# A tile's rounding, the signs of others and some sums of blocks change places between block 0 and block 2

## The chip, the cores and the metric

The kernel runs on one core of a Trainium2 chip. The core has five engines that run beside each other, each through its own list of instructions in order: TensorE (PE, matrix products), VectorE (DVE), ScalarE (ACT), GpSimd (POOL) and SyncE (SP, which here only issues DMAs). They wait for one another through semaphores. The metric is the device time of one execution in microseconds, as the median of several runs.

## What is computed

Linear attention over 8 batches of 8 heads (576 positions, 64 dimensions) is normalised, its heads are laid side by side into x (4608 x 512), and a two-layer network with a leaky ReLU follows:

```python
kv = np.einsum('bhsd,bhse->bhde', k, v)
out = np.einsum('bhsd,bhde->bhse', q, kv)
rms = np.sqrt(np.mean(out * out, axis=-1, keepdims=True) + 1e-06)
x = (out / rms * g_norm)        # heads side by side: 4608 x 512
h = x @ w_in                    # 512 x 2048
g = np.maximum(0.01 * h, h)
out = g @ w_out                 # 2048 x 512
```

q, k, v and the result are float32. w_in and w_out arrive as float64 and are rounded to float32 on the chip.

## The kernel before

**Blocks and units.** The 4608 rows of x are nine blocks of 512. The hidden width of 2048 is four chunks c = 0 to 3. Block 0 is computed for its first three chunks in a plain way (`first_block`, 12 steps: product h_ps, the ReLU L1139 on ACT, then product o_acc one step later). Then comes a list of units, each one chunk of one block: block 1 with chunks 0 to 3 (units 0 to 3), block 0 with chunk 3 (unit 4), and then blocks 2 to 8 with four chunks each. A unit computes both matrix products by Strassen's scheme, seven products in place of eight, in the order 1, 2, 6, 5, 7, 3, 4 (`ORDER`). Products 5, 6, 7 and 3 or 4 need sums of operand blocks: those of w_in (`sides_w1`, on POOL, into `pairs`), of x (`sides_x`, on DVE), of g (`sums_of`, on POOL, into `gs`) and of w_out (`sides_w2`, on POOL). From block 2 on the first product is split by Strassen a second time; the sums for that come from `combine` (POOL, into `stage`, then by DMA to a copy in DRAM) and from `inner` (POOL).

**The loop and its slots.** Each unit has seven slots t = 0 to 6, one for each product of h. In a slot the generator of h gives one product (PE, and the instruction on ACT or DVE that reads it); two slots behind, the generator of o gives one of the unit before. After that the slot issues stored-up DMAs (`write_later`), sums on POOL (`combine`), pieces of a tile's rounding, loads, and pieces of the attention for later blocks (`a_steps`). Nearly all instructions are pinned, so that the order of the lines is the order on each engine, and DMAs on SP are issued in that order too.

**Rounding.** The weights come as 32 tiles of 128 x 512 float64 values (`w_jobs`). One tile's rounding (`round_f64`) is a chain across two engines: ACT add (L264), ACT cut (L262), DVE clamp (L266), ACT sign and scale (L271, "the sign" below), DVE L281, DVE L284. It is a generator with a stop after each of these and one empty stop ahead of L271. In block 0, `round_w` takes the first three steps and leaves the rest to `finish_w`, written as f in the plan of steps; a number in the plan is a tile, a is one step of block 1's attention, t one of its leftover from block 0, and x makes all four sums of block 1's x at once (L1174). In a plan key (n, half), half 0 stands before the o_acc of the step before, half 1 after it. Tiles 27 to 31 are rounded in the loop, three slots each. A tile is loaded by SP into one of a few places (`early`, `stage`, `pairs`) once an earlier tile there has been read.

**POOL's entry into block 1.** L1193 copies one element of x's last sum into `pairs`, so POOL begins block 1 only when the four sums are done. It then makes, in order: the four sums of w_in for unit 0, two of w_out, eight for combine(0, 0) and combine(0, 1), two more of w_out; and then within the loop those of the next unit.

Of the kernel before, what the change touches and what calls it, by code (L numbers as in the profile page):

```python
# [24 lines left out]
def kernel(  # L25
# [754 lines left out]
    def combine(c, part):  # L780


        direct = w1_sb[0][c].rearrange("p u (t r) m -> p u r t m", t=2)
        last = w1_sb[1][c][:, :, 2:, :].unsqueeze(3)
        parts = [((5, 6), pair(0, U, 2, 2, P))], [((7, 3), pair(1, U, 2, 2, P))], \
            [((1, 2), direct), ((4,), last)]

        for js, y in parts[part]:
            t = view(next(stage_homes), 0, 4, len(js), P)
            s1, s2, s3, s4 = (t[:, i, :, :] for i in range(4))  # L790
            y11, y12, y21, y22 = (y[:, u, r, :, :] for u in range(2) for r in range(2))

            add(nc.gpsimd, s1, y21, y22)
            add(nc.gpsimd, s2, s1, y11, True)
            add(nc.gpsimd, s3, y11, y21, True)
            add(nc.gpsimd, s4, y12, s2, True)
            to = w1_dram[c][:, :, AT[js[0]]:AT[js[0]] + len(js), :]
            if js[0] == 1:
                for r in range(2):
                    put_off(to[:, r, :, :], y[:, 0, r, :, :], 2 - part // 2)  # L800
            else:
                put_off(to[:, :2, :, :], y[:, 0, :, :, :], 2 - part // 2)
            put_off(to[:, 2, :, :], y22, 2 - part // 2)
            put_off(to[:, 3:, :, :], t, 2 - part // 2)
# [291 lines left out]
    def go(steps, n=None):  # L1096
        while n is None or n > 0:
            if next(steps, steps) is steps:
                return
            n = None if n is None else n - 1  # L1100
# [20 lines left out]
    def first_block(between):  # L1121
# [27 lines left out]
        for t in range(4):  # L1149
# [10 lines left out]
    plan = {(1, 0): (5, f, t), (1, 1): (t, 6, f, t), (2, 0): (t, 7, f, t), (2, 1): (8, f, t, t),  # L1160
            (3, 0): (9, f, t, a), (3, 1): (10, f), (4, 0): (11, f, a), (4, 1): (12, f),
            (5, 0): (13, f, a), (5, 1): (14, f), (6, 0): (15, f), (6, 1): (16, f),
            (7, 0): (a, a, 17, f), (7, 1): (a, 18, f), (8, 0): (a, 19, 24, f), (8, 1): (a, 20, f),
            (9, 0): (a, a, 21, f), (9, 1): (22, a, f, a), (10, 0): (a, 23, f, a), (10, 1): (x, 25, f),
            (11, 0): (26, f)}
    loaded, x_sides = 12, None

    def between(n, half):
        nonlocal loaded, x_sides
        for what in plan.get((n, half), ()):  # L1170
            if what == f:
                finish_w()
            elif what == x:
                x_sides, _, sums, _ = sides_x(1)  # L1174
                go(sums)
            elif what in (t, a):
                go(tail if what == t else a_steps, 1)
            else:
                round_w(what)
                to = what + 7 if what < 17 else {23: 26, 25: 28, 26: 28}.get(what, 25)  # L1180
                while loaded <= min(to, 31):
                    load_w(loaded)
                    loaded += 1
                    if loaded in (13, 16):
                        load_pair(1, {13: 2, 16: 3}[loaded], homes=homes_1[{13: 2, 16: 3}[loaded]])
# [11 lines left out]
    for part in range(2):  # L1197
# [2 lines left out]
    in_loop = True  # L1200

    LATE_ONE = {15: 2, 16: 2, 17: 1, 18: 1, 19: 2}
    A_SLOTS = {18: 1, 19: 2, 22: 1, 23: 1, 24: 1, 25: 1, 26: 1, 27: 1, 28: 2, 29: 1, 30: 1, 31: 2,
               34: 2}
    DIRECT = {23: 0, 25: 1, 27: 2, 29: 3}
    READS = {28: 2, 30: 4, 32: RING}
# [27 lines left out]
    for i, chunks in rounds:  # L1234
        one = in_block_1 = i < 2
        steady = not one
        if i == 1:
            late, a_steps = a_steps, attention(2)
        elif i > 1:
            late, a_steps = a_steps, attention(i + 1, fine=True) if i + 1 < B else iter(())  # L1240
        os = {}
        for c in chunks:
            now += 1
            nxt = units[now + 1] if now + 1 < len(units) else (NB, 0)
            g_sides = {}
            h_steps = product_h(now, h_sides, x_sides, g_sides) if one else \
                product_h_two(i, c, now, quarters, g_sides, second_of(now - 2))
            for t in range(7):
                slot = 7 * c + t
                if rest:  # L1250
                    go(steps, rest[0][0])
                go(h_steps, 1)
                if not one:

                    if t == 6:
                        go(h_steps, 1)
                    if slot in LATE_SLOTS:
                        go(late, 1)
                    for _ in range(FINE_SLOTS.get(slot, 0)):
                        go(a_steps, 1)  # L1260
                    if i + 1 < NB:
                        if slot == 20:
                            x_sides, new_quarters, sums, inner = sides_x(i + 1)
                        if slot in (20, 21, 22):
                            go(sums, 2 if slot == 20 else 1)
                        if slot == 24:
                            inner(0)
                        elif slot == 25:
                            inner(1)
                    load_some()  # L1270

                if now - 1 in seconds:
                    for half in range(2):
                        if t == (6 if half else 4):
                            inner_g(now - 1, half)
                    if t == 5 and now - 1 < 2 * NC + NC - K:
                        inner_w2(units[now - 1][1])
                if (7 * now + t == 7 * NC + 4):
                    while writes:
                        pin(nc.sync.dma_start(*writes.pop()))  # L1280
                if slot in HELD and i == NB - 1:
                    pass
                elif waited == LAG:
                    go_o()
                elif o_queue:
                    waited += 1
                write_later()
                at = 7 * now + t
                for key in PARTS.get(at, ()):
                    if at == 33:  # L1290
                        part_os = os
                    load_part(part_os, key)
                if at in READS:
                    read(READS[at])
                if one:
                    if at in DIRECT:
                        combine(DIRECT[at], 2)
                    if t == 3 and nxt[0] < 2 and nxt[1] != c:
                        h_sides, more_h = sides_w1(nxt[1])
                        combine(nxt[1], 0)  # L1300
                    if t == 5 and nxt[0] < 2 and nxt[1] != c:
                        more_h()
                        combine(nxt[1], 1)
                    if not rest and rounded < len(w_jobs):
                        steps = rounding(rounded)
                        rest.extend(((0, 3), (2, 1), (0, 1)))
                        rounded += 1
                    if rest:
                        go(steps, rest.popleft()[1])
                    if loaded < min(rounded + 2, len(w_jobs)):  # L1310
                        load_w(loaded)
                        loaded += 1
                    if at in (15, 16):
                        load_pair(2, at - 15)
                    go(late, LATE_ONE.get(at, 0))
                    go(a_steps, A_SLOTS.get(at, 0))
                    load_some(2 if at in (19, 20) else 1)
                    if at == 7 * NC - 4:
                        x_sides, _, sums, _ = sides_x(0)
                    elif at == 7 * N1 - 3:  # L1320
                        x_sides, new_quarters, sums, inner = sides_x(2)
                    if at in (7 * NC - 4, 7 * NC - 3, 7 * N1 - 3, 7 * N1 - 2):
                        go(sums, 2)
                    if at == 7 * N1 - 2:
                        inner(0)
                    elif at == 7 * N1 - 1:
                        inner(1)

            for _ in range(2 if i == NB - 1 and c == NC - 1 else 0):
                go(h_steps, 1)  # L1330
                go_o()
            go(h_steps)
            if c == NC - 1 and i != 1 and i + 1 < NB:
                inner(2)
                quarters = new_quarters
            by_two = NC + NC - K <= now < len(units) - 2
            if by_two:
                seconds[now] = (os, store(i))
            o_queue.append(product_o(now, g_sides, os, store(i), by_two))
# [32 lines left out]
```

## Time and profile before

| | us |
|---|---|
| median of 3 runs | 929.04 |
| lowest and highest | 926.89, 932.18 |
| the profiled execution's own time | 930.66 |
| its span, first to last instruction | 929.0 |
| PE busy | 910.7 (98%) |
| DVE busy | 610.2 (66%) |
| ACT busy | 347.5 (37%) |
| POOL busy | 390.6 (42%) |

The granted clock of TensorE was 0.994 of full speed in the mean. PE is busy nearly all the time, so the profile is read for the few places where it isn't, and for what ends each of those waits. A busy PE that runs at a lower granted clock counts as busy too, so the length of a group of products has to be compared with that of its like. In a row of the timeline the first number is the start, the second the length to the last visible end; a bracket gives the idle time of the engine before it and what ended that.

### The profile page before, as it was taken

What the parts mean: (1) busy time and instruction counts of PE and PEld (TensorE: products, weight loads), DVE (VectorE), ACT (ScalarE), POOL (GpSimd) and SP (SyncE); (2) the same over time, 40 slices, a digit from 0 to 9 for tenths busy, and PEclk for the clock granted to TensorE, in tenths of its full rate; (3) what the DMA queues carried; (4) which work ended last, traced back from release to release, by engine and by line L of the source; (5) the groups of instructions that cost most, each with busy time, mean ns of one, the idle gap of its engine ahead of it and who ended that gap; (6) DMA issues with size and microseconds to landing.
All of it is one profiled execution on the core that took longest, in us unless ns stands there. A gap on an engine that the chain in (4) does not pass through costs nothing.

```text
span 929.0 us, 18151 instructions
## 1 busy us (share of the span) xinstructions
PE 910.7 (98%) x7024; PEld 785.7 (85%) x7024; DVE 610.2 (66%) x1119; ACT 347.5 (37%) x679; POOL 390.6 (42%) x475
## 2 busy tenths in 40 slices
PE   8999798999999999999999999999999999999998
PEld 4544367888898999999999999999999999999997
DVE  5765872554565877577756785688658755765565
ACT  5756543213334422433243324433343333223330
POOL 2000189898452275226322632254325522552322
PEclk9999999999999999999999999999999999999999
DMA  8998255797989678867886788757765676667633
GB/s 252 230 249 215 68 196 185 206 301 224 292 273 324 224 227 252 261 218 234 245 263 224 226 206 270 241 168 223 240 185 172 192 223 198 184 188 218 198 119 91
DMA packets 92405, 202.16 MB, mean 218 GB/s; under 512 B 10016, under 2 KB 44448, under 8 KB 92320
## 3 DMA queue, kind: packets, MB, share of 16 engines
q1 hardware_dynamic: 81344, 189.14, 69.0%
q10 hardware_dynamic: 10528, 10.69, 3.4%
q8 instruction: 56, 0.92, 0.4%
q0 software_dynamic: 448, 1.18, 0.3%
q14 instruction: 29, 0.24, 0.1%
HBM read 173.44 MB, written 27.53 MB: 216 GB/s over the span
## 4 chain that ended last, share of the span: by engine, by line
PE 82%; DMA 9%; POOL 3%; DVE 3%; issue 1%; ACT 1%; SPq 0%; POOLq 0%; ACTq 0%; DVEq 0%
PE o_c L126 19%; PE o_a L126 18%; PE h_ha L126 11%; PE h_hb L126 10%; PE h_hc L126 8%; PE h_hd L126 8%; DMA pairs<-in_moe_w_in_dram 3%; PE o_ps L126 3%; DMA stage<-in_moe_w_in_dram 2%; POOL stage L698 2%; PE h_a L126 2%; POOL pairs L698 1%; PE h_c L126 1%; DMA pairs<-in_v_dram 1%; PE h_b L126 1%
## 5 line engine op out<-in xcount | busy, mean ns | idle before, releaser
L698 POOL TENSOR_TENSOR gs<-g 128x512 f32<-128x512 f32 x66 | 84.3, 1278 | 249.1 <-ACT g L909 249.1
L909 ACT ACTIVATE g<-g 128x512 f32<-128x512 f32 x127 | 80.1, 631 | 143.0 <-DVE g L698 143.0
L1028 ACT COPY w_all<-h_ha 128x512 f32<-128x512 f32 x84 | 48.9, 582 | 171.3 <-PE h_ha L126 165.6
L126 PE MATMUL o_a<-pairs,gs 128*128 128x256 f32 x392 | 93.6, 381 | 2.6 <-POOL gs L698 2.6
L126 PE MATMUL o_c<-pairs,gs 128*128 128x256 f32 x392 | 93.2, 381 | 0.0
L698 DVE TENSOR_TENSOR o<-o_a,o 128x512 f32<-128x512 f32 (+1 forms) x93 | 62.7, 674 | 34.3 <-PE o_a L126 33.8
L698 DVE TENSOR_TENSOR o<-h_hb,o 128x128 f32<-128x128 f32 x104 | 29.9, 287 | 83.0 <-ACT pairs L1028 82.9
L126 PEld LDWEIGHTS o_a<-pairs,gs 128*128 128x128 f32 x392 | 71.4, 191 | 11.0 <-POOL gs L698 3.0
L126 PEld LDWEIGHTS o_c<-pairs,gs 128*128 128x128 f32 x392 | 71.3, 190 | 9.5 <-POOL pairs L698 1.2
L698 DVE TENSOR_TENSOR o<-o_c,o 128x512 f32<-128x512 f32 x80 | 54.8, 685 | 32.9 <-PE o_c L126 32.7
L126 PE MATMUL h_ha<-stage,w_all 128*128 128x128 f32 x448 | 59.9, 276 | 1.7 <-POOL stage L698 1.7
L126 PEld LDWEIGHTS h_ha<-stage,w_all 128*128 128x128 f32 x448 | 56.7, 192 | 4.8 <-POOL stage L698 1.9
L698 DVE TENSOR_TENSOR g<-g,pairs 128x512 f32<-128x512 f32 x84 | 55.7, 689 | 1.9
L698 POOL TENSOR_TENSOR pairs<-g 128x128 f32<-128x128 f32 x52 | 23.7, 456 | 77.1 <-PE h_hb L126 48.5
L126 PE MATMUL o_acc<-w,g 128*128 128x512 f32 x96 | 46.7, 632 | 6.0 <-ACT g L1139 6.0
L698 DVE TENSOR_TENSOR w_all<-h_hc,w_all 128x512 f32<-128x512 f32 x56 | 38.4, 685 | 15.8 <-PE h_hc L126 15.8
L698 DVE TENSOR_TENSOR o<-h_hd,o 128x128 f32<-128x128 f32 x78 | 22.2, 284 | 38.1 <-ACT pairs L1028 38.0
L126 PE MATMUL h_hb<-stage,w_all 128*128 128x128 f32 x336 | 46.7, 275 | 0.0
L698 POOL TENSOR_TENSOR gs<-gs,g 128x512 f32<-128x512 f32 x33 | 44.5, 1348 | 2.6
L1028 ACT COPY pairs<-h_hb 128x384 f32<-128x384 f32 x84 | 40.0, 476 | 13.6 <-PE h_hb L126 13.1
L1193 POOL COPY pairs<-xt 1x1 f32<-1x1 f32 x1 | 0.2, 177 | 106.7 <-DVE xt L698 106.7
L698 POOL TENSOR_TENSOR gs<-g,gs 128x512 f32<-128x512 f32 x33 | 45.0, 1362 | 0.0
(237 smaller groups left out, 2273.9 us busy)
## 6 DMA issues: line engine op xcount, KB each, us to landing
w_all<-w SPq DMA_DIRECT2D x196, 448.0 KB, 4.2
pairs<-w SPq DMA_DIRECT2D x56, 512.0 KB, 4.3
out_dram<-o ACTq DMA_DIRECT2D x35, 256.0 KB, 4.6
v_in<-in_v_dram SPq DMA_DIRECT2D x27, 288.0 KB, 4.7
k_in<-in_k_dram SPq DMA_DIRECT2D x26, 288.0 KB, 4.4
q_in<-in_q_dram SPq DMA_DIRECT2D x52, 144.0 KB, 5.5
q_in<-in_q_dram SPq DMA_DIRECT2D x52, 140.0 KB, 5.4
w<-stage SPq DMA_DIRECT2D x12, 512.0 KB, 4.2
```

Source lines behind the costliest of these rows:

```text
L126: pin(nc.tensor.matmul(*args, **kw))
L698: ins = eng.tensor_tensor(out_, a, b_, op=ALU.subtract if minus else ALU.add)
L909: first_turn(nc.scalar.activation(t, t if src is None else src, func=AF.Prelu, alpha=SLOPE))
L1028: nc.scalar.copy(q[:, at], bank)
L1193: pin(nc.gpsimd.tensor_copy(pair(0, NW)[:1, :1], x_sides[4][:1, 0, :1]))
```

## The change

Four things move; no instruction's kind or size changes.

- In the plan for block 0, tile 25 leaves step (10, 1) for (8, 1), where it stands with tile 20. The step (10, 1) then holds x's four sums alone. In (9, 1) the attention step comes ahead of tile 22's rounding, and `finish_w` behind a second attention step. The table of loads lets tiles 26 to 28 be issued after tile 22 already.
- In the loop, a tile's second piece was split: the sign (L271) was issued at the start of the slot, ahead of the product's own instructions, and L281 at its end. Now both stand at the end, behind the instructions of the slot's products.
- combine(c, 1) of the next chunk stood in slot 5 of the unit before; now it stands in slot 0 of its own unit, behind that unit's predecessor's sums of g. Its three writes to DRAM move with it, behind the loads of q, k and v that SP issues there.
- x's sums of block 2 and `inner` of the first two kinds come one slot earlier, and so do some steps of the attention (`A_SLOTS`).

```diff
-            (7, 0): (a, a, 17, f), (7, 1): (a, 18, f), (8, 0): (a, 19, 24, f), (8, 1): (a, 20, f),
-            (9, 0): (a, a, 21, f), (9, 1): (22, a, f, a), (10, 0): (a, 23, f, a), (10, 1): (x, 25, f),
-            (11, 0): (26, f)}
+            (7, 0): (a, a, 17, f), (7, 1): (a, 18, f), (8, 0): (a, 19, 24, f),
+            (8, 1): (a, 20, 25, f), (9, 0): (a, a, 21, f), (9, 1): (a, 22, a, f),
+            (10, 0): (a, 23, f, a), (10, 1): (x,), (11, 0): (26, f)}
...
-                to = what + 7 if what < 17 else {23: 26, 25: 28, 26: 28}.get(what, 25)
+                to = what + 7 if what < 17 else {22: 28, 23: 28, 26: 28}.get(what, 25)
...
-    A_SLOTS = {18: 1, 19: 2, 22: 1, 23: 1, 24: 1, 25: 1, 26: 1, 27: 1, 28: 2, 29: 1, 30: 1, 31: 2,
+    A_SLOTS = {18: 1, 19: 2, 22: 1, 23: 1, 24: 2, 25: 1, 26: 1, 27: 2, 28: 1, 29: 1, 30: 1, 31: 1,
...
-                if rest:
-                    go(steps, rest[0][0])
                 go(h_steps, 1)
...
-                        combine(nxt[1], 1)
+                    if t == 0 and units[now - 1][1] != c and now > 0:
+                        combine(c, 1)
...
-                        rest.extend(((0, 3), (2, 1), (0, 1)))
+                        rest.extend((3, 3, 1))
...
-                        go(steps, rest.popleft()[1])
+                        go(steps, rest.popleft())
...
-                    elif at == 7 * N1 - 3:
+                    elif at == 7 * N1 - 4:
                         x_sides, new_quarters, sums, inner = sides_x(2)
-                    if at in (7 * NC - 4, 7 * NC - 3, 7 * N1 - 3, 7 * N1 - 2):
+                    if at in (7 * NC - 4, 7 * NC - 3, 7 * N1 - 4, 7 * N1 - 3):
                         go(sums, 2)
-                    if at == 7 * N1 - 2:
+                    if at == 7 * N1 - 3:
                         inner(0)
-                    elif at == 7 * N1 - 1:
+                    elif at == 7 * N1 - 2:
                         inner(1)
```

## The prediction

> **What bounds the kernel now.** Times are microseconds from the span's start; products are named by Strassen number as in the section on the kernel. I read the waits of PE first. After 250 it waits for nothing, so a gain must come from the start of block 1. Waits of PE between 100 and 160:
>
> ```profile
> PE o_acc L126 <- ACT g L1139: 6.0, 2, 5.4
> PE o_a L126 <- POOL gs L698: 2.6, 1, 2.6
> PE h_b L126 <- ACT g L934: 1.3, 1, 1.3
> PE h_a L126 <- DVE g L698: 0.2, 1, 0.2
> ```
>
> PE's timeline there:
>
> ```profile
> 101.04 3.67 PE L126 MATMUL h_ps<-xT,w_all 128*128 128x512 f32 x8
> 105.31 3.70 PE L126 MATMUL o_acc<-w,g 128*128 128x512 f32 x8 [0.60 <-ACT g L1139]
> 114.43 6.67 PE L126 MATMUL o_acc<-w,g 128*128 128x512 f32 x8 [5.42 <-ACT g L1139]
> ...
> 138.40 1.97 PE L126 MATMUL h_b<-xt,pairs 128*128 128x256 f32 x8 [1.28 <-ACT g L934]
> ...
> 149.85 2.53 PE L126 MATMUL o_a<-pairs,gs 128*128 128x256 f32 x8 [2.57 <-POOL gs L698]
> ```
>
> The stalls sum to 9.5 (5.42, 0.21, 1.28, 2.57). Two cost more: o_acc after the first takes 6.67 instead of 3.60 (3.07 lost), and the two products after the last end 1.95 late (155.25 in the chain, against 149.85 and twice 1.727). So 14.5 is lost. Why is g late? ACT's timeline:
>
> ```profile
> 107.20 0.63 ACT L271 ACTIVATE w<-cut 128x512 int32<-128x512 f32 x1 [0.81 <-DVE cut L266]
> ...
> 113.26 0.63 ACT L271 ACTIVATE w<-cut 128x512 int32<-128x512 f32 x1 [4.29 <-DVE cut L266]
> 113.80 0.58 ACT L1139 ACTIVATE g<-h_ps 128x512 f32<-128x512 f32 x1
> ```
>
> The sign (L271) of tile 25 waits for its clamp, which DVE does at 112.81, after x's four sums; the last g of block 0 stands behind it. The second question is what the same stretch costs POOL:
>
> ```profile
> 113.12 0.18 POOL L1193 COPY pairs<-xt 1x1 f32<-1x1 f32 x1 [106.72 <-DVE xt L698]
> 113.42 1.27 POOL L698 TENSOR_TENSOR pairs<-w_all 128x512 f32<-128x512 f32 x1
> ...
> 130.70 1.45 POOL L698 TENSOR_TENSOR pairs<-w,pairs 128x512 f32<-128x512 f32 x1
> 134.21 1.28 POOL L698 TENSOR_TENSOR pairs<-w_all 128x512 f32<-128x512 f32 x1 [2.06 <-DMA w<-pairs]
> 135.57 1.27 POOL L698 TENSOR_TENSOR pairs<-pairs,w_all 128x512 f32<-128x512 f32 x1
> ...
> 148.09 1.70 POOL L698 TENSOR_TENSOR gs<-gs,g 128x512 f32<-128x512 f32 x1
> ```
>
> POOL starts only when x's last sum is done (112.21 to 112.90 on DVE) and then hardly rests. PE's stall hides that POOL is nearly as late: the h_b at 138.40 needs POOL's 135.57 instruction, done at 136.84. That decides my forecast.
>
> [...] granted clock 0.50 from 114 to 120, and from 152 to 154 after a stall of only 2.57. [...] from 113.42 to 132.15 POOL's 14 instructions took 18.73, where the same forms take 16.09 [...] (171.9 to 180 and 152 to 157); 9 rounding instructions of DVE fell in, so 0.29 each.
>
> **Tile 25 earlier.** It landed before 89.3 (the DMA share is nil from there to 96). ACT gets its add and cut at 93.34 and 93.91 (0.57 each). DVE: clamp of tile 20 at 93.56 as before, of 25 at 94.60; ACT signs 20 at 94.48, 25 at 95.04; DVE then has L281, L284 of both (0.66 wait, 0.72, 0.61, 0.72, 0.61), so the transpose of 96.01 starts at 97.80: +1.79. ACT's g moves from 94.55 to 95.57; its o_acc runs at 97.61, so that is hidden.
>
> From there DVE sets the pace: tile 21's clamp 100.22, sign 100.67, last step (L284) 102.06, clamp of 22 at 102.67, reciprocal 103.02. With the step of the division now inside tile 22's rounding, spread is at 103.43, sign of 22 at 104.37, L284 105.75, then transpose 106.36, product 107.03, clamp of 23 at 108.15, sum 108.51, sign 108.60, L284 109.98, transpose 110.59, product 111.26, sums 112.39, 113.00, 113.60. The last sum was at 112.21: **+1.39**. POOL's first addition moves from 113.42 to 114.81.
>
> PE: h_ps of 101.04 needs tile 21, hence starts near 102.8; o_acc waits for tile 22 (106.5); the last g is at 109.14, so the last o_acc starts when tile 23 is done, 110.72, and ends at 114.15 instead of 120.94. Block 1's first product is **6.8 earlier**, at full clock. This doesn't stay.
>
> **Signs at the slot's end.** L934 of h_b's first product no longer stands behind a sign: the 1.28 goes. Earlier, within unit 0, product 6 waits for POOL's second sum (114.81 + 1.35 + 1.55 = 117.7), product 5 for a DVE addition behind tile 27's clamp (about 121.4), product 4 for one behind 28's; unit 0 ends near 129.2, and the next two products near 132.6. None of this matters if POOL is later still.
>
> **POOL to unit 1's sums.** 132.15 + 1.39 = 133.54 for the same instructions with as many of DVE's among them. The 2.06 wait for the write of pairs goes: tile 27 is read by 118.0, so SP issues tile 29's four loads to 120.3, the parts to 122.1, waits for POOL (124.1), issues three writes (2.9), and with the 3.5 of the flight the place is free at 130.6, 2.9 before it is wanted. Two additions of 2.69 [...] (tile 29's rounding now overlaps) give 136.4 to 136.8; I take **136.55** for the h_b that ran at 138.40: 1.85 earlier. PE idles some 4.0 before it, and pays the clock: between 1.95 (after 2.57) and 3.07 (after 5.42), by length **2.5**. Five products (8.63): unit 0's o_a with sums of g is asked for at 147.7.
>
> **Sums of blocks behind those of g.** POOL after 136.5: four of 256 wide (2.86 to 3.9), two additions (2.57), two sums of g (2.58 to 3.45): 144.5 to 146.4, in time. With the four of combine still ahead (2.9) it would be 147.4 to 149.3, so this edit is worth 0 to 1.6. The moved four and their three DMAs (now behind block 2's loads on SP) are wanted much later: at 152.20 POOL took the pair of unit 2, which PE used at 167.87.
>
> So o_a starts at 147.7, the product two later at 151.15 instead of 155.25: **4.1 earlier**.
>
> **Attention steps and x of block 2 one slot earlier.** Same instructions; o_ps keeps one product between kv and itself (kv ends 201.76, copies 0.48). POOL's inner sums didn't wait for x: at 244.28 it waited 2.94 for a DMA that SP held for an out_dram store, whose data come from PE's o_c at 238.58. So PE's 1.67 at 248.04 stays; bounds: a gain of all 1.67, a loss of one DVE addition, 0.7. I take 0. Tiles 26 to 28 load earlier into idle queues: 0.
>
> **Sum.** 929.0 − 4.1 = 924.9 for the span; the profiled run took 930.66, 1.66 outside the span, while the median of the runs is 929.04. I apply the 4.1 to the median: **924.9**.
>
> **Rivals.**
> - *POOL isn't the bound*: all 14.5 come back, 914.5. For: PE's largest stall is named after ACT. Against: POOL's row at 134.21, and 113.42, which moves later. Half of it (about 920) needs [...] 16.09 instead of 18.73.
> - *POOL and the clock keep more of it*: [...] the sums of g late: gain 2, 927. [...]
> - *Slower*: tile 25 lands late. ACT and DVE take their work in order, so behind it stand tile 21, the division, x's sums and POOL; each us past 93.3 is a us at unit 1's h_b. The 4.1 is used up when it lands at 97.4; at 102 the kernel takes 933.7. Against: the DMA share, nil from 89.3.
>
> **Numbers.** Forecast (gain 3 to 5.5) 0.60, half or more of the stalls 0.12, gain below 3 but not slower 0.20, slower 0.08. The forecast's own range is 923.5 to 926. Each bound is widened by 1.5 for the runs' spread (926.89 to 932.18): 921.0 to 928.8. A measurement can tell about 0.5% (4.65) from no change, and the forecast lies just inside it: faster 0.44, same 0.48, slower 0.08.
>
> **What would show it.** Right: no ACT g L1139 among PE's long waits, last o_acc near 110.7 lasting about 3.6; POOL's L1193 at 114.5; PE's longest wait in 100 to 160 is unit 1's h_b for POOL pairs, 3 to 5, followed by half clock; POOL without a wait for w<-pairs; no wait for gs. Wrong: L1193 at or before 113, or that h_b before 134.5 or after 138; a wait of PE after 155 that was not there.

## The result and the profile after

The changed kernel takes 925.85 us (median of 20 runs, 924.15 to 930.64) against 930.64 of the kernel before (20 runs on the same chip): a ratio of 0.9956, 95% interval 0.9940 to 0.9971. That is 4.1 us by the ratio, 4.8 by the medians. The profiled executions have spans of 929.0 and 925.1. Waits of PE between 100 and 160 in the changed kernel (in all, times, longest):

```profile
PE h_b L126 <- POOL pairs L698: 4.8, 1, 4.8
PE h_ps L126 <- DVE w_all L284: 2.0, 1, 2.0
PE h_c L126 <- DVE g L698: 1.2, 1, 1.2
```

The wait of 5.42 for ACT's g is gone, and so is the wait for the sums of g. The longest is now one for POOL. PE's timeline of the changed kernel (start, length, instruction, in brackets the wait ahead of it):

```profile
102.83 5.40 PE L126 MATMUL h_ps<-xT,w_all 128*128 128x512 f32 x8 [1.98 <-DVE w_all L284]
108.07 7.03 PE L126 MATMUL o_acc<-w,g 128*128 128x512 f32 x16
114.93 1.89 PE L126 MATMUL h_a<-xT,w_all 128*128 128x256 f32 x8
...
130.26 1.89 PE L126 MATMUL h_d<-xT,w_all 128*128 128x256 f32 x8
136.93 3.78 PE L126 MATMUL h_b<-xt,pairs 128*128 128x256 f32 x8 [4.78 <-POOL pairs L698]
140.50 2.54 PE L126 MATMUL o_a<-w,g 128*128 128x256 f32 x8
142.88 1.89 PE L126 MATMUL h_d<-xt,pairs 128*128 128x256 f32 x8
...
148.06 1.89 PE L126 MATMUL o_a<-pairs,gs 128*128 128x256 f32 x8
...
151.51 1.89 PE L126 MATMUL o_c<-pairs,gs 128*128 128x256 f32 x8
```

Block 1's first product starts at 114.93, where it was 120.94: 6.0 earlier. At unit 1's h_b only 1.47 of that is left (136.93 against 138.40), because PE stands still for 4.78 in front of it and then runs at a lower clock (0.50 granted from 137.0 to 140.5, 0.73 from there to 142.88): h_b and o_a take 3.57 and 2.38 to the next start instead of 1.727, 2.50 lost. No wait follows, so the first o_c on sums of g starts at 151.51 where it was 155.09. POOL's timeline in the changed kernel:

```profile
114.43 0.18 POOL L1193 COPY pairs<-xt 1x1 f32<-1x1 f32 x1 [108.04 <-PE o_acc L126]
114.73 1.27 POOL L698 TENSOR_TENSOR pairs<-w_all 128x512 f32<-128x512 f32 x1
...
132.09 1.44 POOL L698 TENSOR_TENSOR pairs<-w,pairs 128x512 f32<-128x512 f32 x1
133.50 1.71 POOL L698 TENSOR_TENSOR pairs<-w_all 128x512 f32<-128x512 f32 x1
135.28 1.59 POOL L698 TENSOR_TENSOR pairs<-pairs,w_all 128x512 f32<-128x512 f32 x1
...
143.58 1.28 POOL L698 TENSOR_TENSOR gs<-gs,g 128x512 f32<-128x512 f32 x1
```

POOL works without a pause from 114.73 on; the wait for the write of `pairs` (2.06 before) is gone. The releaser named at L1193 is an inference: that o_acc is merely the last semaphore to change. What lets POOL go is x's last sum on DVE, 113.52 to 114.20. ACT and DVE show why that is later and block 0's last g earlier. ACT, with both signs of tiles 20 and 25 in one row, and the last g:

```profile
94.50 1.25 ACT L271 ACTIVATE w<-cut 128x512 int32<-128x512 f32 x2
...
109.05 0.57 ACT L1139 ACTIVATE g<-h_ps 128x512 f32<-128x512 f32 x1
```

DVE, the transpose that follows tile 25's rounding, and x's last sum:

```profile
97.83 0.64 DVE L430 STREAM_TRANSPOSE turned<-sum 128x448 f32<-128x448 f32 x1
...
113.52 0.68 DVE L698 TENSOR_TENSOR xt<-xT,xt 128x512 f32<-128x512 f32 x1
```

At the start of block 2 one wait is a little shorter. Before, then after:

```profile
248.04 0.94 PE L126 MATMUL h_ha<-stage,w_all 128*128 128x128 f32 x6 [1.67 <-POOL stage L698]
```

```profile
244.23 0.94 PE L126 MATMUL h_ha<-stage,w_all 128*128 128x128 f32 x6 [1.44 <-POOL stage L698]
```

So 3.58 is won by o_c and 0.23 here, 3.8 of the 3.9 that the span is shorter.

### The profile page after: what moved, and what is told of

Its sections match the earlier page's. It is cut to its first block, busy times and chain, and to the rows that moved or that the text cites. A ratio compares the mean times of both kernels' runs of the same rounds, so it can differ in the third digit from the quotient of the medians.

```text
span 925.1 us, 18145 instructions
## 1 busy us (share of the span) xinstructions
PE 909.7 (98%) x7024; PEld 786.1 (85%) x7024; DVE 610.7 (66%) x1119; ACT 347.6 (38%) x679; POOL 392.9 (42%) x475
## 4 chain that ended last, share of the span: by engine, by line
PE 84%; DMA 9%; POOL 2%; DVE 2%; issue 1%; ACT 1%; SPq 0%; POOLq 0%; ACTq 0%; DVEq 0%
PE o_c L126 19%; PE o_a L126 18%; PE h_ha L126 11%; PE h_hb L126 10%; PE h_hc L126 8%; PE h_hd L126 8%; DMA stage<-in_moe_w_in_dram 3%; PE o_ps L126 2%; DMA pairs<-in_moe_w_in_dram 2%; DMA q_in<-in_q_dram 2%; PE h_b L126 2%; PE h_a L126 2%; POOL pairs L698 1%; PE h_c L126 1%; POOL stage L698 1%
## 5 line engine op out<-in xcount | busy, mean ns | idle before, releaser
L698 POOL TENSOR_TENSOR gs<-g 128x512 f32<-128x512 f32 x66 | 84.0, 1272 | 249.5 <-ACT g L909 249.5
L698 DVE TENSOR_TENSOR o<-h_hb,o 128x128 f32<-128x128 f32 x104 | 29.9, 287 | 83.2 <-ACT pairs L1028 83.1
L698 DVE TENSOR_TENSOR o<-o_a,o 128x512 f32<-128x512 f32 (+1 forms) x93 | 62.7, 674 | 30.4 <-PE o_a L126 30.1
L698 DVE TENSOR_TENSOR o<-o_c,o 128x512 f32<-128x512 f32 x80 | 54.8, 686 | 31.8 <-PE o_c L126 31.7
L698 DVE TENSOR_TENSOR g<-g,pairs 128x512 f32<-128x512 f32 x84 | 55.7, 689 | 1.9
L698 POOL TENSOR_TENSOR pairs<-g 128x128 f32<-128x128 f32 x52 | 23.8, 457 | 75.7 <-PE h_hb L126 47.4
L698 DVE TENSOR_TENSOR w_all<-h_hc,w_all 128x512 f32<-128x512 f32 x56 | 38.4, 685 | 15.8 <-PE h_hc L126 15.5
L698 DVE TENSOR_TENSOR o<-h_hd,o 128x128 f32<-128x128 f32 x78 | 22.2, 284 | 38.2 <-ACT pairs L1028 38.0
L126 PE MATMUL h_ps<-xT,w_all 128*128 128x512 f32 (+1 forms) x104 | 45.0, 580 | 2.0 <-DVE w_all L284 2.0
L1193 POOL COPY pairs<-xt 1x1 f32<-1x1 f32 x1 | 0.2, 177 | 108.0 <-PE o_acc L126 108.0
L698 POOL TENSOR_TENSOR gs<-g,gs 128x512 f32<-128x512 f32 x33 | 45.2, 1369 | 0.0
L698 POOL TENSOR_TENSOR gs<-gs,g 128x512 f32<-128x512 f32 x33 | 44.1, 1335 | 2.6
```

The source lines that it names most:

```text
L126: pin(nc.tensor.matmul(*args, **kw))
L698: ins = eng.tensor_tensor(out_, a, b_, op=ALU.subtract if minus else ALU.add)
L1193: pin(nc.gpsimd.tensor_copy(pair(0, NW)[:1, :1], x_sides[4][:1, 0, :1]))
```

## The experiments

**A common zero.** Loads of the weights land at different times from one execution to the next, even of one kernel: ACT's cut (L262) of tile 24, which can't begin before its load has landed, starts between 86.01 and 91.66 in the profiles here, and all of block 1 shifts with it: from that cut to L1193 it is 24.50 in each of the three profiles with tile 25 in its old place (before, e1, e12), and 25.76 to 25.88 in the nine with tile 25 moved and POOL's entry unchanged. So two profiles are compared by the time from that instruction to a later one, below "from tile 24". Unless a section says otherwise, each kernel is the changed one with one edit. The times are medians, the ratios are to the kernel before on the same chip; the chips differ between experiments, so times in different rows compare less well than ratios. Each row's stage is from one profile.

| kernel | tile 24's cut | unit 1's h_b (its wait) | wait for sums of g | first o_c on sums of g | from tile 24: h_b, o_c | time | ratio, 95% interval |
|---|---|---|---|---|---|---|---|
| before | 88.62 | 138.40 (1.28) | 2.57 | 155.09 | 49.78, 66.47 | 930.64 | |
| changed | 88.66 | 136.93 (4.78) | 0 | 151.51 | 48.27, 62.85 | 925.85 | 0.9956, 0.9940 to 0.9971 |
| e1: tile 25 back | 88.64 | 136.34 (1.07) | 0.78 | 149.58 | 47.70, 60.94 | 925.18 | 0.9955, 0.9941 to 0.9968 |
| e2: tile 25 alone | 87.70 | 136.09 (4.89) | 0.95 | 151.15 | 48.39, 63.45 | 926.40 | 0.9973, 0.9961 to 0.9985 |
| e3: sums back | 86.55 | 134.92 (4.78) | 0.90 | 149.97 | 48.37, 63.42 | 927.22 | 0.9970, 0.9957 to 0.9983 |
| e4: signs back | 89.55 | 137.93 (4.91) | 0 | 151.52 | 48.38, 61.97 | 926.23 | 0.9952, 0.9934 to 0.9969 |
| e5: x of block 2 back | 86.01 | 134.35 (4.77) | 0 | 148.23 | 48.34, 62.22 | 926.10 | 0.9958, 0.9947 to 0.9970 |
| e6: POOL from x's first sum | 86.08 | 135.00 (0.90) | 0 | 147.16 | 48.92, 61.08 | 923.44 | 0.9941, 0.9920 to 0.9962 |
| e7: w_out's second sums later | 89.05 | 133.98 (1.43) | 2.57 | 151.43 | 44.93, 62.38 | 925.90 | 0.9954, 0.9938 to 0.9970 |
| e8: idle products | 86.21 | 134.60 (0.48) | 0 | 146.79 | 48.39, 60.58 | 923.54 | 0.9928, 0.9910 to 0.9946 |
| e9: e6 and idle products | 91.66 | 140.01 (0) | 0 | 152.10 | 48.35, 60.44 | 928.24 | 0.9986, 0.9972 to 1.0001 |
| e10: changed again | 86.41 | 134.77 (4.77) | 0 | 148.64 | 48.36, 62.23 | 925.46 | 0.9968, 0.9952 to 0.9984 |
| e11: idle products again | 90.38 | 138.65 (0.47) | 0 | 150.84 | 48.27, 60.46 | 924.83 | 0.9934, 0.9916 to 0.9953 |
| e12: before, idle products | 90.58 | 139.17 (2.00) | 2.57 | 155.86 | 48.59, 65.28 | 930.75 | 1.0019, 1.0003 to 1.0036 |

One column tells most. With tile 25 in its new place and POOL's order up to unit 1's sums of w_in unchanged (changed, e2, e3, e4, e5, e8, e10, e11), unit 1's h_b comes 48.27 to 48.39 after tile 24, whatever else is edited, and its wait is for POOL. e10 against "changed" (62.23 and 62.85 to o_c) shows what two executions of one kernel differ by.

### e1 and e2: is PE's longest wait the bound, or POOL?

e1 is the changed kernel with the old plan and the old table of loads; e2 is the kernel before with the new ones and nothing else.

```diff
# e1, from the changed kernel (e2 is the same edit the other way round, from the kernel before)
-            (8, 1): (a, 20, 25, f), (9, 0): (a, a, 21, f), (9, 1): (a, 22, a, f),
-            (10, 0): (a, 23, f, a), (10, 1): (x,), (11, 0): (26, f)}
+            (8, 1): (a, 20, f), (9, 0): (a, a, 21, f), (9, 1): (22, a, f, a),
+            (10, 0): (a, 23, f, a), (10, 1): (x, 25, f), (11, 0): (26, f)}
...
-                to = what + 7 if what < 17 else {22: 28, 23: 28, 26: 28}.get(what, 25)
+                to = what + 7 if what < 17 else {23: 26, 25: 28, 26: 28}.get(what, 25)
```

> The changed kernel with tile 25 back in step (10, 1), the other edits kept. Theory (POOL sets when unit 1 goes on; tile 25 only moves the stall): the 5.4 before the last o_acc comes back with its slow clock, x's last sum and POOL's start go back to 112.2 and 113.1, POOL waits about 2 for w<-pairs again, and unit 1's h_b (product 6) starts at 137.0 with no stall of its own over 0.5; sums of g are ready at 146.0 to 146.8; the first o_c<-pairs,gs starts at 149.5 to 150.3, where the changed kernel has 151.5. So this run is 1 to 2 us faster than the changed kernel, about 924. Rival (the move of tile 25 is the gain): the 5.4 and the 3.1 of clock are paid in full, o_c at 157 or later, 931 or more.

> The kernel before with only the plan of block 0 changed (tile 25 beside 20, its loads). Theory: POOL starts at 114.7 as in the changed kernel, unit 1's h_b waits 4 to 5 for POOL pairs and starts at 136.9 to 137.5, the slow clock costs 2.5, sums of g with combine ahead are ready near 147.9, so the o_a on them starts at 148 to 148.6 and o_c<-pairs,gs at 151.5 to 152.0. This edit alone gives 3 to 3.6 us, nearly the whole 4. Rival (each edit gives its own stall): 8.5 us from this edit, 920.5.

PE's timeline in e1:

```profile
114.46 5.27 PE L126 MATMUL o_acc<-w,g 128*128 128x512 f32 x8 [5.42 <-ACT g L1139]
119.57 1.89 PE L126 MATMUL h_a<-xT,w_all 128*128 128x256 f32 x8
...
136.34 1.99 PE L126 MATMUL h_b<-xt,pairs 128*128 128x256 f32 x8 [1.07 <-POOL pairs L698]
...
146.02 1.99 PE L126 MATMUL o_a<-pairs,gs 128*128 128x256 f32 x8 [0.78 <-POOL gs L698]
...
149.58 1.89 PE L126 MATMUL o_c<-pairs,gs 128*128 128x256 f32 x8
```

The largest wait of the kernel before is back, whole, with block 1's first product 4.6 later than in the changed kernel, and o_c is not later at all: it is 1.9 earlier. PE waits either early (5.42 for ACT, then 1.07 for POOL) or late (4.78 for POOL). The other edits do the rest: the wait for the sums of g is 0.78 in place of 2.57 and without a slower clock behind it (that o_a takes 1.83 to the next start, where it took 2.32), and h_b comes 2.1 earlier than in the kernel before. Of that, 1.5 goes with the sign's edit, read from these rows: h_b starts 0.05 behind the end of POOL's second sum of w_in (136.29), where in the kernel before it starts 1.56 behind it (136.84), as L934 stands behind a sign there. POOL's own part is some 0.6: its wait for the write of pairs is 1.17 in place of 2.06. The rival, that the last g must come early, expected 157 or more and falls. In the runs e1 (0.9955) and the changed kernel (0.9956) don't differ, so the 1 to 2 expected there didn't show.

In e2 tile 25 alone wins 3.0 from tile 24 to o_c (66.47 to 63.45) and 0.27% in the runs. The two parts, 5.5 and 3.0, give 3.6 to 4.2 together. They don't add because they win the same things: each alone has h_b start right behind POOL's sum, and each takes most of the same wait for the sums of g (2.57 becomes 0.78 in e1 and 0.95 in e2), which can go only once. With tile 25 moved, the slow clock behind h_b's wait is paid as well: h_b takes 3.48 to the next start in e2, 1.84 in e1.

### e12: a clock loss of PE ahead of POOL's bound

If POOL sets the time of unit 1's h_b, then the half clock that follows the 5.42 in the kernel before (0.50 granted from 114 to 120, 3.07 lost) costs nothing either. Idle products in that wait take it away and leave the wait:

```diff
# from the kernel before, in first_block
             between(n, 0)
+            if n == 2 * K * U:
+                warm_ps = ps_att.tile([P, NT], F32, tag="att", name="warm_ps")
+                for _ in range(12):
+                    matmul(warm_ps[:, :N2], lhsT=w1_sb[0][0][:, 0, 0, :],
+                           rhs=x[:, 0, :N2], start=True, stop=True)
```

> The kernel before, with twelve idle products of 256 columns (of no use to the result) in its longest wait, ahead of the last o_acc; the wait for tile 25 itself stays. Theory (POOL's pairs are the bound of the stretch, so what PE loses ahead of them counts for nothing): the last o_acc still starts at 114.4 but takes 3.6 instead of 6.7, block 1's first product is 3.1 earlier, unit 1's h_b is at 136.9 to 138.4 as before and waits 2.8 to 4.4 in place of 1.3, then loses some 2 to the clock; the first o_c on sums of g within 1 of 155.1; a time of 929.5, ratio 0.999 to 1.001. Rival (every stall and every slow clock of PE is paid in full): the 3.07 comes back, o_c at 152.0, 926.4, ratio 0.9967.

PE's timeline in e12:

```profile
110.81 5.34 PE L126 MATMUL warm_ps<-xT,w_all 128*128 128x256 f32 x24
116.39 3.70 PE L126 MATMUL o_acc<-w,g 128*128 128x512 f32 x8 [0.23 <-ACT g L1139]
119.93 1.89 PE L126 MATMUL h_a<-xT,w_all 128*128 128x256 f32 x8
...
139.17 1.97 PE L126 MATMUL h_b<-xt,pairs 128*128 128x256 f32 x8 [2.00 <-ACT g L934]
...
150.61 2.68 PE L126 MATMUL o_a<-pairs,gs 128*128 128x256 f32 x8 [2.57 <-POOL gs L698]
...
155.86 1.89 PE L126 MATMUL o_c<-pairs,gs 128*128 128x256 f32 x8
```

The last o_acc takes 3.54 to the next start instead of 6.51. From L1193 on POOL (115.08 here, 113.12 in the kernel before) to block 1's first product it is 4.85 instead of 7.82, all of the 3.0 won; to o_c it is 40.78 instead of 41.97, only 1.2 less. And this 1.2 is POOL's: the wait of 2.06 for the write of pairs isn't there in e12, more of POOL's sums take longer (those at 132.84 and 134.54 took 1.73 each, their like before 1.45 and 1.28), and its second sum of g ends 35.48 after L1193 where it ended 36.67. PE starts on it at once in both (149.79 to 149.85, and 150.56 to 150.61), after the same wait of 2.57. So none of PE's 3.0 reaches o_c.

h_b is named after ACT in both kernels, yet it starts 1.56 behind the end of POOL's second sum of w_in in both. DVE and ACT in the kernel before:

```profile
135.62 1.50 DVE L266 TENSOR_SCALAR cut<-cut 128x512 f32<-128x512 f32 x1 [1.72 <-ACT cut L262]
...
137.69 0.57 ACT L934 COPY g<-h_b 128x512 f32<-128x512 f32 x1
```

POOL, DVE and ACT in e12:

```profile
134.54 1.73 POOL L698 TENSOR_TENSOR pairs<-w_all 128x512 f32<-128x512 f32 x1
136.34 1.26 POOL L698 TENSOR_TENSOR pairs<-pairs,w_all 128x512 f32<-128x512 f32 x1
...
148.86 1.70 POOL L698 TENSOR_TENSOR gs<-gs,g 128x512 f32<-128x512 f32 x1
...
136.35 1.53 DVE L266 TENSOR_SCALAR cut<-cut 128x512 f32<-128x512 f32 x1 [1.23 <-ACT cut L262]
...
138.46 0.57 ACT L934 COPY g<-h_b 128x512 f32<-128x512 f32 x1
```

The clamp (L266), which takes 0.42 while POOL is idle (106.74 in the kernel before), runs beside POOL's sum and ends 0.28 after it; the sign, L934 and h_b follow. That POOL's sum holds the clamp up is inferred from these times.

The runs show no gain (1.0019). Taken alone they don't settle it, since e12's profile also loses 2.7 more than the kernel before at the start of block 2 (see e9); the stage does. The rival put o_c 3.07 earlier and falls, since it is 1.2.

### e8 and e11: the price of the slow clock behind the longest wait

```diff
                 slot = 7 * c + t
+                if now == 1 and t == 2:
+                    warm_ps = ps_att.tile([P, NT], F32, tag="att", name="warm_ps")
+                    for _ in range(10):
+                        matmul(warm_ps[:, :N2], lhsT=w1_sb[0][0][:, 0, 0, :],
+                               rhs=x_sides[1][:, 0, :], start=True, stop=True)
                 go(h_steps, 1)
```

> The changed kernel with ten products of 256 columns (0.43 each, into an unused bank, read by nobody) on PE ahead of unit 1's h_b product 6, so that PE is busy while it waits for POOL. Theory (the stall also costs the clock): h_b starts at the same time, 136.9 with tile 24 landed at 88.1, but at full clock, 1.73 long; o_a on the sums of g 2.5 earlier, at 145.6, o_c<-pairs,gs at 149.0: 2.5 us faster than the changed kernel. Rival (h_b is slow for another reason, for instance POOL's traffic): no gain.

> The changed kernel with ten idle products of 256 columns ahead of unit 1's product 6, once more, to see whether its lead over the changed kernel is there again. Theory (the slow clock after the longest wait costs 2.5): a ratio to the kernel before of 0.993 (0.9956 and 0.9968 were measured for the changed kernel), unit 1's h_b at full clock after a wait under 1 us. Rival (the first look was a lucky draw of loads): 0.996.

PE's timeline in e8:

```profile
129.64 4.48 PE L126 MATMUL warm_ps<-xT,w_all 128*128 128x256 f32 x20
134.60 1.99 PE L126 MATMUL h_b<-xt,pairs 128*128 128x256 f32 x8 [0.48 <-POOL pairs L698]
136.43 1.89 PE L126 MATMUL o_a<-w,g 128*128 128x256 f32 x8
...
146.79 1.89 PE L126 MATMUL o_c<-pairs,gs 128*128 128x256 f32 x8
```

h_b comes no earlier (48.39 after tile 24), but h_b and o_a are done in 3.56 instead of 5.95. From L1193 to o_c it is 34.70 in e8 and 34.69 in e11, where the two profiles of the changed kernel have 37.08 and 36.36 (e10): 2.4 or 1.7 won. In the runs the two reach 0.9928 and 0.9934 where the changed kernel has 0.9956 and 0.9968. Of the four pairs of intervals three still overlap a little, but the order is the same in all, and by their ratios these two are the fastest of all versions here, some 2 to 3.7 ahead of the changed kernel and 6 to 7 ahead of the kernel before.

### e7: POOL's work for unit 1 ahead of work that is wanted later

```diff
     for part in range(2):
         combine(0, part)
-    sides_w2(0)[1](1)
     in_loop = True
...
+                        if now == 0:
+                            sides_w2(0)[1](1)
                         combine(nxt[1], 0)
```

> The changed kernel with POOL's two sums of w_out of the second kind for unit 0 (2.64 us on POOL) behind unit 1's first two sums of w_in instead of ahead. Theory: unit 1's h_b starts 2.6 earlier, at 134.3, with a stall near 2.1 and 0 to 2 of slow clock; sums of g are ready at 144.9 as before; o_a on them at 144.9, o_c<-pairs,gs at 148.3, 3.2 us faster than the changed kernel, about 922.5. Rival (h_b waits for something that POOL does not set): no change, 925.9.

PE's timeline in e7:

```profile
133.98 2.00 PE L126 MATMUL h_b<-xt,pairs 128*128 128x256 f32 x8 [1.43 <-POOL pairs L698]
...
146.18 3.28 PE L126 MATMUL o_a<-pairs,gs 128*128 128x256 f32 x8 [2.57 <-POOL gs L698]
...
151.43 1.89 PE L126 MATMUL o_c<-pairs,gs 128*128 128x256 f32 x8
```

h_b comes 3.3 earlier from tile 24 (2.6 was expected), and takes 1.83 to the next start instead of 3.57. It is all given back at o_a: POOL still has the same list ahead of the sums of g, so PE waits 2.57 there and the slow clock follows there: o_a and h_d take 3.08 and 2.17 to the next start instead of 1.727, 1.8 lost. Of the 3.2 expected at o_c at most 0.5 is left (62.38 against 62.85 and 62.23). In the runs e7 (0.9954) doesn't differ from the changed kernel. Moving work within POOL's list, all of it ahead of the sums of g, didn't move the end here.

### e6 and e9: POOL enters block 1 earlier

```diff
# e6
-    pin(nc.gpsimd.tensor_copy(pair(0, NW)[:1, :1], x_sides[4][:1, 0, :1]))
+    pin(nc.gpsimd.tensor_copy(pair(0, NW)[:1, :1], x_sides[5][:1, 0, :1]))
# e9: as e6, and in the loop
+                if now < 2 and t == 2:
+                    warm_ps = ps_att.tile([P, NT], F32, tag="att", name="warm_ps")
+                    for _ in range(8 - 4 * now):
+                        matmul(warm_ps[:, :N2], lhsT=w1_sb[0][0][:, 0, 0, :],
+                               rhs=x_sides[1][:, 0, :], start=True, stop=True)
```

> The changed kernel, L1193 reads x's first sum in place of the last, so POOL may begin some 5 us earlier. Theory (POOL's start is the bound): L1193 near 109.4, POOL's second sum for unit 1 at 133 to 134 (5.3 earlier[...]), unit 1's h_b waits under 1.5, no slow clock; sums of g near 141.6, o_a on them near 142.3, o_c<-pairs,gs at 145 to 147 instead of 151.5: 5 to 6 us faster than the changed kernel, about 920. DVE's x sums end 3 to 5 later. Rival [...]: x's sums and tile 26 late, unit 0 late, h_b still at 136 or later, 925 or more.

> The changed kernel, with two things together: POOL enters block 1 on x's first sum instead of its last, and TensorE computes idle products (of no use to the result) in two of its waits, 8 of 256 columns ahead of unit 0's product 6 and 4 ahead of unit 1's. Theory (POOL's eight pairs are one bound, and a stall costs its length and then a slow clock, which idle products prevent): with tile 24 loaded as early as in the fastest runs, POOL enters at 106.8, the first product 6 still starts near 118.8 but at full clock, unit 1's h_b near 132.7, the first o_a on sums of g near 142.2 (there POOL's sums of g are the next limit), the first o_c on sums of g near 145.6, about 1.2 earlier than with idle products alone; a time of about 922.5. Rival ([...] what POOL gains at its entry is lost in x's sums): no better than idle products alone, 923.5 to 924.

DVE's timeline in e6, x's second to fourth sum:

```profile
110.16 1.64 DVE L698 TENSOR_TENSOR xt<-xT,xt 128x512 f32<-128x512 f32 x1
111.72 1.75 DVE L698 TENSOR_TENSOR xT<-xT 128x512 f32<-128x512 f32 x1
113.39 1.75 DVE L698 TENSOR_TENSOR xt<-xT,xt 128x512 f32<-128x512 f32 x1
```

POOL enters at 106.76, but three of x's sums now take 1.64 to 1.75 in place of 0.68 each, beside POOL's additions, which take 1.72 to 2.00 there. That is the price, 3.1 for three sums; that the additions hold them up is inferred from the times (in e9, with the same entry, they take 1.64, 1.75 and 1.75). Tile 26's clamp stands behind them on DVE, its sign waits for the clamp on ACT, and L934, which reads unit 0's first product, stands behind the sign. ACT's timeline, then PE's:

```profile
116.58 0.63 ACT L271 ACTIVATE w<-cut 128x512 int32<-128x512 f32 x1 [8.37 <-DVE cut L266]
...
118.06 0.60 ACT L934 COPY g<-h_a 128x512 f32<-128x512 f32 x1
```

```profile
118.76 3.75 PE L126 MATMUL h_a<-xt,pairs 128*128 128x256 f32 x8 [3.44 <-issue]
```

Unit 0's product 6 starts 0.10 behind L934, after 3.44 of waiting, and at a lower clock: it and the next product take 3.54 and 3.00 to the next start instead of 1.727. That L934 releases it is inferred from the times, as the profile names no engine. So h_b comes 48.92 after tile 24, a little later than without the edit, and no longer waits for POOL, whose sum ended at 132.63, 2.4 before it; what is won (1.1 to 1.8 to o_c) is the slow clock that h_b no longer has (1.80 to the next start, where it was 3.57), not the 5 to 6 expected of POOL's entry. In the runs e6 (0.9941) doesn't stand clear of the changed kernel. e9 adds idle products in both waits. o_c is then 60.44 after tile 24, 0.1 better than with idle products alone, not 1.2. The reason stands in its timeline: PE goes from h_d through the second set of idle products to h_b without a pause (136.56, 138.28, 140.01), while POOL was done at 137.67. The four filled a wait that was no longer there, and cost up to 1.7. In its runs e9 is 0.9986, the worst of all versions of the changed kernel. In its profile the loss lies at the start of block 2:

```profile
246.61 1.65 PE L126 MATMUL h_ha<-stage,w_all 128*128 128x128 f32 x6 [2.48 <-POOL stage L698]
248.05 1.49 PE L126 MATMUL h_hb<-stage,w_all 128*128 128x128 f32 x6
249.47 2.20 PE L126 MATMUL kv_ps<-v_in,k_in 64*64 64x64 f32 x72
251.59 2.40 PE L126 MATMUL o_a<-w,g 128*128 128x256 f32 x8
```

Two waits of 0.47 and 2.48 stand where the changed kernel has 1.44, and a slow clock follows, which costs 2.6 more: h_ha, h_hb and kv_ps are 1.65, 1.49 and 2.20 long, in the changed kernel 0.94, 0.88 and 1.28. e12 shows the same (2.49, then 0.99, 1.49 and 2.14). In both, POOL waits longer there for a copy of `stage` in DRAM (5.10 and 4.45, against 2.79 in the changed kernel). Why that copy came later in these two is open; no run changed it alone.

### e3, e4 and e5: the other three edits, each undone

```diff
# e3: combine(c, 1) back in slot 5 of the unit before
                         more_h()
+                        combine(nxt[1], 1)
-                    if t == 0 and units[now - 1][1] != c and now > 0:
-                        combine(c, 1)
# e4: the sign back at the slot's start
+                if rest:
+                    go(steps, rest[0][0])
                 go(h_steps, 1)
...
-                        rest.extend((3, 3, 1))
+                        rest.extend(((0, 3), (2, 1), (0, 1)))
# e5: x's sums of block 2, inner and A_SLOTS back (as in the kernel before)
-                    elif at == 7 * N1 - 4:
+                    elif at == 7 * N1 - 3:
...
```

> The changed kernel with combine(c, 1) back in slot 5 of the unit before, ahead of the sums of g. Theory (POOL's order matters only as far as the sums of g pass 148.1, when PE asks for them): POOL's second sum of g ends 2.9 later, near 147.8 to 148.5, so PE waits 0 to 0.8 for gs and o_c<-pairs,gs starts 0 to 0.8 later than the 151.5 of the changed kernel (with the same landing of tile 24): no difference in the runs. Rival (this edit gives the 2.6 of gs and its slow clock): 2 to 4.5 us slower than the changed kernel.

> The changed kernel with the signs of tiles 27 to 31 back at the slot's start. Theory: unit 1's h_b waits for POOL in any case, so a sign ahead of L934 costs nothing there: o_c<-pairs,gs within 0.5 of 151.5, no difference in the runs. Rival (this edit gives the 1.3): 1.3 us slower.

> The changed kernel with x's sums of block 2, the inner sums and the attention steps where they were before. Theory: POOL's inner sums wait for a DMA there, not for x: PE's wait for stage near 244 stays between 1.3 and 1.8, no difference in the runs. Rival: 0.7 or more slower or faster.

With the sums of blocks back ahead of those of g, the wait for gs returns. PE's timeline in e3:

```profile
146.41 1.99 PE L126 MATMUL o_a<-pairs,gs 128*128 128x256 f32 x8 [0.90 <-POOL gs L698]
```

This edit is worth 0.9 in the stage; in the runs (0.9970) it doesn't stand clear of the changed kernel. The signs (e4) and block 2's x (e5) cost nothing that can be measured: h_b waits for POOL in any case, and PE's wait at block 2's start is 1.50 in e5, 1.44 with the edit. Each was undone only beside tile 25's move. By e1 these three edits give the whole gain without that move; how it divides among them there is open, as no run has one of them alone on the kernel before.

### e10: the changed kernel once more

> The changed kernel once more, as the measure for the run beside it on the same chip: 925.9, a ratio to the kernel before of 0.9956; from POOL's entry into block 1 to the first o_c on sums of g 37.1, unit 1's h_b waiting 4.8 for POOL.

The changed kernel gave a ratio of 0.9968 and a median of 925.46 this time. From L1193 to o_c it is 36.4, with 1.8 lost to the clock, in place of 2.5, behind the same wait of 4.77. The 1.8 is the usual size: e2, e3, e4 and e5, with waits of 4.77 to 4.91, lose 1.5 to 1.8.

## Why the prediction was right

**The bound.** Right: PE's stall hid that POOL was nearly as late. "Block 1's first product 6.8 earlier; this doesn't stay" became 6.0 earlier, and 1.5 of it at h_b. The rival with all 14.5 back falls with e12, where none of the 3.0 that PE gains ahead of POOL's bound reaches o_c, and with e1, where the stall of 5.42 is back and nothing is lost.

**Tile 25 earlier.** DVE's transpose was put at 97.80 and x's last sum at 113.60; they are at 97.83 and 113.52. POOL's first addition was put at 114.81 and is at 114.73, the last g at 109.14 and is at 109.05. Not foreseen: the h_ps that had to wait for tile 21 (102.83, as worked out) ran at a lower clock (0.67 granted), 5.24 to the next start instead of 3.43, so block 1 began 0.8 later than said. It cost nothing, since PE waits for POOL afterwards.

**POOL to unit 1's sums.** 133.54 was worked out for the end of w_out's sums, 133.53 measured, and without a wait for a DMA. (The 18.73 behind it, and the 16.09, are for sixteen sums and not for fourteen; the difference of 2.64 stands. The 0.29 for each of DVE's instructions is an estimate from the two: no run here shows what one of them costs, and from 171.9 to 180 POOL's sums took no longer though DVE was busy for 4.28 of 8.10.) The two additions behind it, put at 3.0, took 3.37 (1.71 and 1.59 with their gap; 1.28 and 1.27 in the kernel before). Both fell beside instructions of DVE (L281 from 133.10, L698 from 134.00, L284 from 134.61 to 135.76); that these made them longer is inferred from the times. So h_b came at 136.93 and not at 136.55. The stall before it was 4.78, not 4.0, because the products before it were done 0.5 sooner than put, and the rest is POOL's 0.4. The clock's price was put at 2.5 between two measured ones and was 2.50; that it hit so exactly is luck, since it was 1.5 to 1.8 in the other five profiles with nearly this wait (e2 to e5, e10).

**Sums of g.** No wait, as said; undone alone (e3) it is 0.90, inside the 0 to 1.6 put for it. **Signs and block 2**: 0 was said, e4 and e5 show 0. PE's wait of 1.67 there became 1.44.

**The sum.** 4.1 was put for o_c, 3.6 measured with 0.2 more at block 2. o_c is at 151.51 and not at 151.15: that is the 0.4 of the two additions, put down above to DVE's instructions beside them. The rest of the difference is a reading: 155.25 for the old o_c comes from the chain, where its row in the timeline starts at 155.09. For the span, 924.9 was worked out and 925.1 measured. That the median of 925.85 came so near to 924.9 is partly luck: the forecast took off 4.1 from 929.04, a median of three, where 20 runs of the kernel before gave 930.64. From there it would have been 926.5, above its own range of 923.5 to 926; the medians differ by 4.8.

What was missed is outside the sum. Most of the working hangs on tile 25's move; e1 shows that without it the runs give the same time, and in its profile o_c even comes 1.9 earlier. The move shifts a wait of PE from the front of POOL's list to its end, and delays POOL's entry by 1.3.

## What to carry to other kernels

Where one engine's list (here POOL's sums) must be done before another engine can go on, removing a stall of the other engine ahead of that point wins nothing by its length: the stall comes back at the point, as 5.42 came back as 4.78, and edits that shorten the same wait don't add. Find the list, and ask what starts it, what runs beside it and gets longer with it (x's sums in e6, 1.64 to 1.75 instead of 0.68), and what in it could stand behind the work that is waited for; check the next point that it serves too, as e7's 3.3 was given back there. Where a wait of TensorE can't be shortened, idle products in it can keep the clock (h_b and o_a together took 3.56 in e8, 5.95 without), but only if the wait is really there, since otherwise they cost their own length, as in e9.

## What was not expected of the hardware

- The clock fell after some waits of about 2 and not after others. An h_ps after a wait of 1.98 took 5.40 (changed kernel, 0.67 granted from 102.83 to 108.07), after 2.43 5.30 (e9), after 2.42 5.18 (e11). But after 2.20 and 2.42 it took 3.70 (e7, e4), and in the kernel before it took 3.67 at 101.04 with the full clock granted (1.00). So the length of the wait alone doesn't decide; what else does, no run here shows.
- The landing of tile 24 differs by 5.6 or more between executions: ACT's add of it waited for the load until 91.09 in e9, and began without a wait at 85.45 in e5. Executions whose loads land late lose nearly all of that time at the start: e11 has the same stage length as e8 (60.46 and 60.58), but its profiled span is 3.8 longer (924.6 and 920.8), with tile 24 4.2 later. Most of the spread of single runs here (924.15 to 930.64 for the changed kernel) may come from this; that is argued from the profiles and not shown for each run.
